# First chunk of sparse attention: exponentials of one sub-chunk moved to ScalarE, value loads reordered, one grouped product split up

## The chip, the cores and the metric

The program runs on one core of a Trainium2 chip. The metric is the device time of one launch in microseconds (us). Three timed runs of the kernel before gave 618.30, 618.59 and 619.15 us; the median is 618.59.

## The reference

For two batches of 576 positions and eight heads of width 64, four heads attend to the last 32 positions ("local") and four to the positions with the same remainder modulo 32 ("strided"), with a softmax in float32. The 1152 x 512 result x then goes through dense products:

```
scores = q @ k.T / 8, masked;  attn = exp(scores - max);  attn /= sum(attn) + 1e-9
x   = attn @ v                                 # 1152 x 512
x   = ((x @ w1) * (x @ w2)) @ w3 @ w_out        # 512 -> 1024 -> 1024 -> 512
out = sum over e of p[:, e] * (relu(x @ e1[e]) @ e2[e])    # 4 experts
```

## The kernel before

The order of the work on every engine is written out by hand, from line 828 on; each engine runs its own instructions in that order and semaphores join them. The change touches the beginning only: the attention of batch 0 and the loads around it.

That attention has six chunks, 0 to 2 local and 3 to 5 strided. For each chunk TensorE (PE) multiplies queries and keys into a PSUM bank (`scores`); VectorE (DVE) takes row maxima (`maxima`, L407), subtracts them into an SBUF frame (`subtract`, L415), ScalarE (ACT) takes exponentials (`exps`, L421), DVE sums and inverts (`sums`, L439 to L445), GpSimd (POOL) multiplies by the inverse (`normalise`, L449). PE transposes the frame (`transposes`, L454), ACT copies the transposes to SBUF (`evac`, L459), PE multiplies them by the values (`pv`, L475, L483 or L492), and ACT copies the products into `x_whole` (`put`, L526). The chunks are staggered, as lines 921 to 974 list them. Batch 1 does the exponentials in another way (`slots_exps`, L423 to L429): ACT reads the scores from PSUM with minus the maximum as its bias, one instruction for each of the six or eight slots, and gives the slot's sum with it.

Chunk 0's product is `paired`: 12 matmuls with 64 x 128 values as weights, of whose result half is used, the first six on one half of the rows and the next six on the other. Chunks 1 and 2 have 24 matmuls on 64 x 64 weights, in turn on the four quarters of the array. A float32 matmul stands as two instructions in the trace.

`keep_warm` (L114) has PE multiply zeros by zeros, so that it is not idle while it waits; nothing reads the result. Two such fillers of 512 columns stand between the first scores.

Nearly all loads are issued by SyncE (SP), in program order, each behind the one before. The queries and keys of the local heads come first (L830, with the queries from ACT's queue), then the values of chunk 0 (three loads), queries and keys of the strided heads (L841), the values of chunks 1 and 2 (four loads) and the strided values (`load_v_str`, `load_v_rest`, L844 and L845). Later, after the scaling of chunk 2, come the first dense weights `w12[0]` in two halves (`whole_load`, L149) and the next weights. `hold` has POOL write one column of a tile, so that the load into it waits for POOL's place in the order.

The dense part follows: `whole_product` (L590) multiplies batch 0's x by `w12[0]` in float32 with no split, in two halves of the weights; each half first takes `whole_low` on ACT and the five `whole_steps` on DVE. The next weights, `w12[1]`, are split in two parts by ACT and DVE, and from L1011 on, `run_unit` does the rest in three products each, with batch 1's attention between them.

Of the kernel before, what the change touches and what calls it, by code (L numbers as in the profile page):

```python
# [14 lines left out]
ALU = mybir.AluOpType  # L15
# [4 lines left out]
W = 32  # L20
# [17 lines left out]
def flat(ap):  # L38
    return ap.rearrange("p a b -> p (a b)")
# [3 lines left out]
def kernel(  # L43
# [13 lines left out]
    nc = tc.nc  # L57
# [14 lines left out]
    def bank(name):  # L72
        return ps.tile([P, 512], F32, tag="ps", name=name)
# [33 lines left out]
    def warm_up():  # L107

        idle = tmp.tile([P, P], F32, tag="pT", name="idle")
        nc.vector.memset(idle, 0.0)  # L110
        nc.scalar.activation(small.tile([P, 1], F32, tag="rec", name="one"), idle[:, :1], AF.Exp)
        moving = idle.unsqueeze(1).to_broadcast([P, 4, P])

        def keep_warm(n):  # L114
            if n:
                acc = bank("idle").rearrange("p (a b) -> p a b", a=4)
            for i in range(n):
                mm(acc, idle, moving, start=i == 0, stop=i == n - 1)

        keep_warm(WARM)  # L120
        return keep_warm
# [6 lines left out]
    class Chunk:  # L128
# [20 lines left out]
        def whole_load(self):  # L149
            nonlocal live  # L150
            live += 1
            self.raw = rawp.tile([P, 1024, 2], I32, tag="raw", name="raw64")
            self.t = unit("w_whole", I32)
            self.f32 = self.t.bitcast(F32)
            hold(True, self.raw[:, 0, :1])
            for i in range(2):
                c = slice(512 * i, 512 * i + 512)
                nc.sync.dma_start(out=flat(self.raw[:, c]), in_=self.src.bitcast(I32)[:, 1024 * i:1024 * i + 1024])

        def whole_low(self, i):  # L160
            c = slice(512 * i, 512 * i + 512)
# [158 lines left out]
                queue.dma_start(out=t[:, :, c], in_=src[b, pairs, :, c].rearrange("k p n -> p k n"))  # L320
        qk[b, g] = (tq, tk)

    def load_v_loc(b, c):

        tv = wp.tile([P, 2, 3, P], F32, tag="w", name="tv_loc")

        def load(dst, rows, t0, n):
            nc.sync.dma_start(out=dst, in_=v_loc[b, :, rows, t0:t0 + n].rearrange("k p t d -> p k t d"))

        lower, upper, middle = slice(0, 64), slice(64, P), slice(W, 3 * W)  # L330
        if c == 0:
            load(tv[lower, :, 0:1], lower, 0, 1)
            load(tv[upper, :, 0:1], middle, 0, 1)
            load(tv[:, :, 1:], slice(0, P), 1, 2)
        elif c == 1:
            load(tv, slice(0, P), 3, 3)
        else:
            load(tv[lower, :, 0:1], lower, 0, 1)
            load(tv[lower, :, 1:], middle, 1, 2)
            load(tv[upper], middle, 3, 3)  # L340
        vals[b, 0, c] = tv
# [11 lines left out]
    def load_v_rest(b):  # L353
        for k in range(2):
            nc.sync.dma_start(out=vals[b, 1][64 * k:64 * k + NB, 10:], in_=v_str[b, k, 2 * T3:2 * T3 + NB, :2])

    class Chunk4:
# [3 lines left out]

        def __init__(self, index, b, g, c):
            self.index, self.b, self.g, self.c = index, b, g, c
            self.paired = b == index == 0
            if g == 0:

                self.blocks = [9 * c + 3 * f + 2 * h if c < 2 else 3 * f + 9 * h + 1 for f in range(3) for h in range(2)]
                self.frames, self.nk = 3, 2 * W
            else:

                if c < 2:
                    self.groups = [(RS[t][0] + 3 * h, 3, 5 * h + t) for t in (2 * c, 2 * c + 1) for h in range(2)]
                else:
                    self.groups = [(RS[4][0] + 3 * h, 3, 5 * h + 4) for h in range(2)]
                    self.groups += [(RS[t][0] + 6, 1, 10 + t) for t in range(2)]
                self.frames, self.nk = 4, T3
            self.slots = 2 * self.frames
# [83 lines left out]
        def pv(self):  # L461

            if self.index == 3 and not self.b:
                banks = [ps_sc.tile([P, 512], F32, tag="sc", name="o") for _ in range(2)]
            else:
                banks = [bank("o") for _ in range(2)]
            if self.paired:
                tv = vals[self.b, 0, self.c]
                self.o = [o[:, :12 * W].rearrange("p (k f j q) -> p k f j q", k=2, f=3, j=2) for o in banks]
                pT = self.pT.rearrange("p (f k j q) -> p f k j q", f=3, k=2, j=2)  # L470
                for h in range(2):
                    r = slice(64 * h, 64 * h + 64)
                    for f in range(3):
                        for k in range(2):
                            mm(self.o[h][:, k, f], tv[r, k, f], pT[r, f, k], start=True, stop=True)  # L475
            elif self.g == 0:
                tv = vals[self.b, 0, self.c]
                self.o = [o[:, :6 * W].rearrange("p (k f q) -> p k f q", k=2, f=3) for o in banks]
                pT = self.pT.rearrange("p (f k j q) -> p f k j q", f=3, k=2, j=2)
                todo = [(f, k, h, j) for f in range(3) for k in range(2) for h in range(2) for j in range(2)]  # L480
                for f, k, h, j in todo:
                    r, d = slice(64 * h, 64 * h + 64), slice(64 * j, 64 * j + 64)
                    mm(self.o[h][d, k, f], tv[r, k, f, d], pT[r, f, k, j], start=True, stop=True)  # L483
            else:
                self.o = [o[:, :self.frames * T3].rearrange("p (f q) -> p f q", q=T3) for o in banks]
                pT = self.pT.rearrange("p (f j q) -> p f j q", j=2, q=2 * W)
                for f, (_, n, at) in enumerate(self.groups):
                    n = NB * n
                    for h in range(2):
                        for j in range(2):  # L490
                            r, d = slice(64 * h, 64 * h + n), slice(64 * j, 64 * j + 64)
                            mm(self.o[h][d, f, :n], vals[self.b, 1][r, at, d], pT[r, f, j, :n], start=True, stop=True)  # L492

        def puts(self):

            t0 = self.b * S
            to = (x_hi, x_lo) if self.b else (x_whole,)
            for h, o in enumerate(self.o):
                if self.g == 0:
                    at = self.blocks[h], self.blocks[2 + h] - self.blocks[h]  # L500
                    x = [x[:, :2, t0:t0 + S].rearrange("p k (i q) -> p k i q", q=W)
                         [:, :, at[0]:at[0] + 2 * at[1] + 1:at[1]] for x in to]
                    if self.paired:
                        for j in range(2):
                            d = slice(64 * j, 64 * j + 64)
                            yield o[d, :, :, j], [x[d] for x in x]
                    else:
                        yield o, x
                else:
                    x = [x[:, 2 + h, t0:t0 + S].rearrange("p (b r) -> p r b", r=W) for x in to]  # L510
                    r0 = self.groups[0][0]
                    parts = o.rearrange("p f (r b) -> p f r b", b=NB)
                    if self.c == 0:
                        for i in range(2):
                            yield (parts[:, 2 * i:2 * i + 2].rearrange("p f r b -> p (f r) b"),
                                   [x[:, 7 * i:7 * i + 6] for x in x])
                    else:
                        n = 4 if self.c == 1 else 2
                        yield parts[:, :n].rearrange("p f r b -> p (f r) b"), [x[:, r0:r0 + 3 * n] for x in x]
                    if self.c == 2:  # L520
                        yield parts[:, 2:, 0], [x[:, 6:14:7] for x in x]
# [306 lines left out]
    with tc.manual_schedule():  # L828
# [8 lines left out]
        make_identity(nc, ident)  # L837
        strided_masks()
        x_whole = big[1].tile([P, 4, S], F32, tag="big", name="x_whole")
        load_v_loc(0, 0)  # L840
        load_qk(0, 1)  # L841
        load_v_loc(0, 1)
        load_v_loc(0, 2)
        load_v_str(0)  # L844
        load_v_rest(0)  # L845
        zero = c_w12[0]
        rest_loads = {5: [lambda: load_qk(1, 1)], 6: [lambda c=c: load_v_loc(1, c) for c in range(3)],
                      8: [lambda: load_v_str(1), lambda: load_v_rest(1)]}
# [58 lines left out]

        def scale_of(i):
            first[i].sums()
            first[i].normalise()  # L910

        def put(i):
# [10 lines left out]
        exp_of(0)  # L923
        keep_warm(1)
        first[2].scores()
        exp_of(1)
        scale_of(0)
        keep_warm(1)
        first[3].scores()
        first[0].transposes()  # L930
        first[4].scores()
        exp_of(2)
        scale_of(1)
        evac(0)
        first[1].transposes()
        first[5].scores()
# [14 lines left out]
        load_next(True)  # L951
        first[3].transposes()
        first[2].pv()
        evac(3)
        put(1)
        first[3].pv()
        scale_of(5)
        load_qk(1, 0, held=True)
# [1 line left out]
        put(2)  # L960
        first[4].transposes()
        evac(4)
        first[5].transposes()
        zero.whole_low(0)
        zero.whole_steps(0)
# [219 lines left out]
```

## Time and profile before

| | |
|---|---|
| median of three runs | 618.59 us |
| the profiled execution | 620.32 us |
| its span, first to last instruction | 618.4 us |
| mean granted clock of TensorE | 0.994 |
| PE busy | 613.7 us, 99% of the span |
| DVE busy, ACT busy | 442.9 us (72%), 278.5 us (45%) |
| POOL busy | 9.8 us |

The page counts an engine as busy while an instruction of its own runs. The granted clock is TensorE's share of its full speed: 1.00 is 2.4 GHz, 0.50 is 1.2 GHz. The chain of waits is followed back from the last instruction, at each step to what released it. All times within the span count from its first instruction.

### The profile page before, as it was taken

How to read it: one execution, taken by the hardware profiler on the slowest of the kernel's cores; microseconds unless marked ns; L12 is line 12 of the kernel's file. 1: busy time of each engine (PE TensorE's matmuls, PEld its weight loads, DVE VectorE, ACT ScalarE, POOL GpSimd, SP SyncE). 2: the span in 40 equal slices, each digit the busy share in tenths (PEclk: the TensorE clock that was granted, in tenths of full speed). 3: DMA queues.
4: the chain of work that ended last, by engine and by line, in shares of the span. 5: the costliest groups of instructions: out<-in, count | busy, mean ns of one | idle time of the engine just before them, and what ended most of it. 6: DMA issues, size and time to landing. Idle time of an engine off the chain costs nothing.

```text
span 618.4 us, 11234 instructions
## 1 busy us (share of the span) xinstructions
PE 613.7 (99%) x4558; PEld 559.5 (90%) x4558; DVE 442.9 (72%) x797; ACT 278.5 (45%) x545; POOL 9.8 (2%) x33
## 2 busy tenths in 40 slices
PE   9999999999999999999999999999999999999997
PEld 5889999998889999999899998899989898989997
DVE  5799986898864236777877987887766665755843
ACT  3779965666643225333343344443333333333320
POOL 4100000000000000000000000000000000000000
PEclk9799999999999999999999999999999999999999
DMA  9987340244523011333445344445585556465411
GB/s 273 315 305 206 112 165 2 77 136 169 196 105 127 32 48 62 136 143 137 166 174 179 121 178 151 166 160 189 187 315 215 208 200 238 170 229 182 146 58 69
DMA packets 28511, 99.64 MB, mean 161 GB/s; under 512 B 2660, under 2 KB 6316, under 8 KB 26028
## 3 DMA queue, kind: packets, MB, share of 16 engines
q1 hardware_dynamic: 27916, 98.34, 45.3%
q8 instruction: 36, 0.59, 0.4%
q10 hardware_dynamic: 544, 0.59, 0.3%
q14 instruction: 15, 0.12, 0.1%
HBM read 79.78 MB, written 19.14 MB: 160 GB/s over the span
## 4 chain that ended last, share of the span: by engine, by line
PE 93%; DVE 3%; DMA 2%; ACT 2%; issue 1%; SPq 0%; DVEq 0%
PE g_acc L303 11%; PE g_acc L304 11%; PE g_acc L305 11%; PE m_a L305 4%; PE m_a L304 4%; PE m_a L303 4%; PE ab_acc L303 3%; PE ab_acc L304 3%; PE ab_acc L305 3%; PE m_b L304 3%; PE m_c L303 3%; PE x_acc L305 3%; PE x_acc L303 3%; PE x_acc L304 3%; PE m_c L304 3%; PE m_b L303 3%
## 5 line engine op out<-in xcount | busy, mean ns | idle before, releaser
L737 ACT ACTIVATE h_hi<-u 128x320 fp32r<-128x320 f32 (+1 forms) x128 | 56.9, 445 | 189.4 <-DVE u L743 189.4
L303 PE MATMUL g_acc<-w_hi,h_hi 128*128 128x512 f32 (+1 forms) x296 | 114.3, 386 | 0.0
L304 PE MATMUL g_acc<-w_lo,h_hi 128*128 128x512 f32 (+1 forms) x296 | 114.2, 386 | 0.0
L305 PE MATMUL g_acc<-w_hi,h_lo 128*128 128x512 f32 (+1 forms) x296 | 113.7, 384 | 0.0
L676 DVE TENSOR_TENSOR w_lo<-raw,w_hi 128x768 fp32r<-128x768 f32 x64 | 69.4, 1084 | 12.4 <-ACT w_hi L674 12.4
L743 DVE TENSOR_TENSOR u<-m_b,u 128x320 f32<-128x320 f32 (+1 forms) x96 | 40.8, 452 | 50.7 <-PE m_b L305 50.6
L303 PE MATMUL ab_acc<-x_hi,w_hi 128*128 128x288 f32 x240 | 71.6, 298 | 0.2 <-ACT ab L578 0.2
L305 PE MATMUL ab_acc<-x_hi,w_lo 128*128 128x288 f32 x240 | 70.7, 294 | 0.0
L304 PE MATMUL ab_acc<-x_lo,w_hi 128*128 128x288 f32 x240 | 70.7, 294 | 0.0
L305 PEld LDWEIGHTS g_acc<-w_hi,h_lo 128*128 128x128 f32 x296 | 55.6, 188 | 11.6
L303 PEld LDWEIGHTS g_acc<-w_hi,h_hi 128*128 128x128 f32 x296 | 55.8, 188 | 8.0
L304 PEld LDWEIGHTS g_acc<-w_lo,h_hi 128*128 128x128 f32 x296 | 55.7, 188 | 7.6
L739 DVE SCALAR_TENSOR_TENSOR h_lo<-u,h_hi 128x320 fp32r<-128x320 f32 (+1 forms) x128 | 57.6, 450 | 3.7 <-ACT h_hi L737 1.9
L674 ACT CAST w_hi<-raw 128x768 fp32r<-128x768 f32 x64 | 59.9, 936 | 0.0
L303 PEld LDWEIGHTS ab_acc<-x_hi,w_hi 128*128 128x128 f32 x240 | 45.0, 188 | 0.7 <-ACT ab L578 0.4
L304 PEld LDWEIGHTS ab_acc<-x_lo,w_hi 128*128 128x128 f32 x240 | 45.0, 188 | 0.0
L305 PEld LDWEIGHTS ab_acc<-x_hi,w_lo 128*128 128x128 f32 x240 | 45.0, 188 | 0.0
L304 PE MATMUL m_b<-b_t,s_hi 128*128 128x320 f32 (+1 forms) x128 | 37.9, 296 | 0.0
L743 DVE TENSOR_TENSOR u<-m_a,u 128x320 f32<-128x320 f32 (+1 forms) x64 | 28.9, 451 | 11.6 <-PE m_a L305 11.6
L676 DVE TENSOR_TENSOR s_lo<-raw,s_hi 128x1024 fp32r<-128x1024 f32 x16 | 19.6, 1226 | 24.3 <-ACT s_hi L674 24.3
L743 DVE TENSOR_TENSOR u<-m_c,u 128x320 f32<-128x320 f32 (+1 forms) x64 | 28.9, 452 | 4.9 <-PE m_c L305 3.9
L753 ACT COPY u<-m_a 128x320 f32<-128x320 f32 (+1 forms) x32 | 12.8, 400 | 41.9 <-PE m_a L305 41.9
(179 smaller groups left out, 1420.4 us busy)
## 6 DMA issues: line engine op xcount, KB each, us to landing
raw<-in_e_dram SPq DMA_DIRECT2D x32, 1024.0 KB, 5.1
raw<-in_w3T_dram SPq DMA_DIRECT2D x8, 1024.0 KB, 5.0
stored<-s_hi SPq DMA_DIRECT2D x16, 512.0 KB, 2.6
stored<-s_lo SPq DMA_DIRECT2D x16, 512.0 KB, 2.7
s_hi<-stored SPq DMA_DIRECT2D x16, 512.0 KB, 3.6
s_lo<-stored SPq DMA_DIRECT2D x16, 512.0 KB, 4.9
raw<-in_w_dram SPq DMA_DIRECT2D x7, 1024.0 KB, 7.2
raw<-in_w_out_dram SPq DMA_DIRECT2D x4, 1024.0 KB, 4.8
```

The lines of the kernel that those rows point to most:

```text
L303: mm(acc, lh, rh, start=first, stop=False)
L304: mm(acc, lh, rl, start=False, stop=False)
L305: mm(acc, ll, rh, start=False, stop=last)
L674: nc.scalar.copy(dst[0], src)
L676: nc.vector.tensor_tensor(out=dst[1], in0=src, in1=dst[0].bitcast(F32), op=ALU.subtract)
L737: nc.scalar.activation(hi, src, AF.Relu)
L739: nc.vector.scalar_tensor_tensor(out=lo, in0=src, scalar=0.0, in1=hi.bitcast(F32), op0=ALU.max, op1=ALU.subtract)
L743: nc.vector.tensor_tensor(out=out, in0=acc, in1=b, op=ALU.add)
L753: nc.scalar.copy(u1, a)
```

## The change

Six edits, all within the first 40 us or so. Chunk 1 of batch 0 takes the way of batch 1 (`slots_exps` on ACT, `recip` afterwards), so its `subtract` and its sum leave DVE, and its reciprocal and scaling come behind `exp_of(2)` in the order. The local values are asked for behind chunk 0's reciprocal: POOL first writes one column of their tile from that reciprocal, so the queries and keys of the strided heads go ahead of them. The strided values are asked for between the two halves of `w12[0]`. Chunk 0's product and its `put` become those of the other local chunks. The second filler has 256 columns, not 512, and a new one of 256 stands between the transposes of chunks 4 and 5. `put(1)` comes ahead of `evac(3)`.

```
-        def keep_warm(n):
+        def keep_warm(n, parts=4):
...
-                mm(acc, idle, moving, start=i == 0, stop=i == n - 1)
+                mm(acc, idle, moving[:, :parts], start=i == 0, stop=i == n - 1)
...
                 nc.sync.dma_start(out=flat(self.raw[:, c]), in_=self.src.bitcast(I32)[:, 1024 * i:1024 * i + 1024])
+                if i == 0:
+                    load_v_str(0)
+                    load_v_rest(0)
...
-    def load_v_loc(b, c):
+    def load_v_loc(b, c, behind=None):
         tv = wp.tile([P, 2, 3, P], F32, tag="w", name="tv_loc")
+        if behind:
+            nc.gpsimd.tensor_tensor(out=tv[:, 0, 0, :1], in0=behind.p[:, 0, :1], in1=behind.rec[:, :1], op=ALU.mult)
...
-            if self.paired:
...
-                for h in range(2):
-                    r = slice(64 * h, 64 * h + 64)
-                    for f in range(3):
-                        for k in range(2):
-                            mm(self.o[h][:, k, f], tv[r, k, f], pT[r, f, k], start=True, stop=True)
-            elif self.g == 0:
+            if self.g == 0:
...
-        load_v_loc(0, 0)
         load_qk(0, 1)
-        load_v_loc(0, 1)
-        load_v_loc(0, 2)
-        load_v_str(0)
-        load_v_rest(0)
...
         def scale_of(i):
             first[i].sums()
+            if i == 0:
+                load_v_loc(0, 0, first[0])
+                load_v_loc(0, 1)
+                load_v_loc(0, 2)
             first[i].normalise()
...
-        exp_of(1)
+        first[1].maxima()
+        first[1].slots_exps()
         scale_of(0)
-        keep_warm(1)
+        keep_warm(1, 2)
...
         exp_of(2)
-        scale_of(1)
+        first[1].recip()
+        first[1].normalise()
...
         first[2].pv()
+        put(1)
         evac(3)
-        put(1)
...
         evac(4)
+        keep_warm(1, 2)
         first[5].transposes()
```

## Rows read from the trace of the kernel before

**Rows 1.** The page, section 2: granted clock of TensorE, in tenths, in 40 slices.
```profile
PEclk9799999999999999999999999999999999999999
```

**Rows 2.** Stretches: us, busy PE, PEld, DVE, ACT, POOL, then granted clock, DMA, GB/s.
```profile
18.00:18.50 0.50, 0.50 (x45) 0.50 (x37) 0.00 (x0) 0.48 (x3) 0.50 (x1) 0.89 0.75 270
...
25.00:26.00 1.00, 1.00 (x37) 0.91 (x34) 0.93 (x4) 1.00 (x6) 0.00 (x0) 0.89 1.00 352
```

**Rows 3.** The chain of waits, 7 to 34 us: start, us, what, how many.
```profile
7.30 1.06 PE idle L118 x2
...
9.33 1.06 PE idle L118 x2
...
14.91 2.43 PE o L475 x24
17.33 0.48 PE tp L454 x3
17.81 0.94 PE o L483 x48
18.75 1.04 PE tp L454 x4
19.80 1.44 PE o L483 x48
21.23 0.89 PE o L492 x32
22.12 1.90 PE tp L454 x8
24.02 1.83 PE o L492 x64
25.85 7.96 PE ab_acc L593 x32
```

**Rows 4.** Waits of PE and of its weight loads: total us, times, longest.
```profile
PE sc L390 <- DMA tqk<-in_qT_dram: 0.3, 1, 0.3
...
PEld sc L401 <- DMA tqk<-in_qT_dram: 0.6, 1, 0.6
```

**Rows 5.** The timeline of DVE, SP and ACT: start, duration, instruction.
```profile
1.74 2.00 SPq L328 DMA_DIRECT2D tv_loc<-in_v_loc_dram  x3
...
8.02 0.56 DVE L415 TENSOR_TENSOR p_ring<-sc,mx 128x384 f32<-128x384 f32 x1
...
10.53 0.54 DVE L439 TENSOR_REDUCE rec<-p_ring 128x6 f32<-128x384 f32 x1
...
10.65 0.52 ACT L421 ACTIVATE p_ring<-p_ring 128x384 f32<-128x384 f32 x1 [1.50 <-DVE p_ring L415]
...
14.75 2.16 SPq L158 DMA_DIRECT2D raw<-in_w_dram  x2
...
18.65 0.33 SPq L138 DMA_DIRECT2D raw<-in_w_dram  x1
...
27.34 1.19 ACT L147 ACTIVATE t<-raw 128x1024 f32<-128x1024 f32 x1
...
35.44 1.35 DVE L552 TENSOR_TENSOR x_lo<-x_whole,x_hi 128x1152 fp32r<-128x1152 f32 x1
```

**Rows 6.** The timeline of ACT, one local chunk of batch 1 by slots.
```profile
47.42 0.20 ACT L425 ACTIVATE mx<-mx 128x6 f32<-128x6 f32 x1
...
49.12 0.34 ACT L428 ACTIVATE p_ring<-sc,mx 128x64 f32<-128x64 f32 x1
```

**Rows 7.** Two stretches of loads, the last column GB/s.
```profile
7.50:10.50 3.00, 3.00 (x54) 1.24 (x53) 2.72 (x7) 0.69 (x2) 0.83 (x1) 1.00 1.07 393
11.50:15.50 4.00, 3.96 (x80) 3.16 (x78) 3.69 (x9) 2.08 (x4) 1.80 (x5) 1.00 1.07 219
```

**Rows 8.** DMA issues of short stretches: KB each, us to landing.
```profile
raw<-in_w_dram SPq DMA_DIRECT2D x1, 512.0 KB, 4.1
...
raw<-in_w_dram SPq DMA_DIRECT2D x1, 1024.0 KB, 6.4
```

More of the change, by code (lines that the diff above doesn't have):

```diff
@@ L112, in warm_up @@
         moving = idle.unsqueeze(1).to_broadcast([P, 4, P])
-        def keep_warm(n):
+        def keep_warm(n, parts=4):
             if n:
-                acc = bank("idle").rearrange("p (a b) -> p a b", a=4)
+                acc = bank("idle").rearrange("p (a b) -> p a b", a=4)[:, :parts]
             for i in range(n):
-                mm(acc, idle, moving, start=i == 0, stop=i == n - 1)
+                mm(acc, idle, moving[:, :parts], start=i == 0, stop=i == n - 1)
         keep_warm(WARM)
@@ L363, in __init__ @@
             self.index, self.b, self.g, self.c = index, b, g, c
-            self.paired = b == index == 0
             if g == 0:
@@ L466, in pv @@
                 banks = [bank("o") for _ in range(2)]
-            if self.paired:
-                tv = vals[self.b, 0, self.c]
-                self.o = [o[:, :12 * W].rearrange("p (k f j q) -> p k f j q", k=2, f=3, j=2) for o in banks]
-                pT = self.pT.rearrange("p (f k j q) -> p f k j q", f=3, k=2, j=2)
-                for h in range(2):
-                    r = slice(64 * h, 64 * h + 64)
-                    for f in range(3):
-                        for k in range(2):
-                            mm(self.o[h][:, k, f], tv[r, k, f], pT[r, f, k], start=True, stop=True)
-            elif self.g == 0:
+            if self.g == 0:
                 tv = vals[self.b, 0, self.c]
@@ L502, in puts @@
                          [:, :, at[0]:at[0] + 2 * at[1] + 1:at[1]] for x in to]
[L503 to L508, printed above, removed]
+                    yield o, x
                 else:
```

## The prediction

> **What bounds the kernel now.** I read the page first: PE is busy for 613.7 of 618.4 us (the table above), and its clock is below nine tenths in one slice of 40, the second [rows 1]. Something to win can therefore only be work that PE need not do or does at half speed, and the second slice, 15 to 31 us, is where to look. The windows show the slow stretch: the clock falls within the half microsecond from 18.0 and is back shortly after 25.0 [rows 2]; by their means of 0.89 it stood at 0.50 from 18.4 to 25.3, that is 6.8 us. The chain of waits shows what PE did there [rows 3]. Before the fall came chunk 0's product, 24 instructions in 2.43 us; chunk 1 does the same sums with 48 instructions in 0.94. The waits list shows that PE hardly stands still for anybody: 0.3 us for the second half of the local queries, 0.6 us of a weight load for the strided ones [rows 4]. Behind the attention the chain is PE again: whole products at 25.85, and then the first split products, just when DVE has done the last part of x, 35.44 + 1.35 = 36.79 us [rows 5].
>
> **The change part by part.** The profiled execution took 620.32 us, 1.92 more than its span and 1.73 more than the median of the runs; I work out a difference within its span and take it off the median. The place that I follow is the start of the whole products, 25.85.
>
> *Chunk 0's product.* 12 wide matmuls become 24 narrow ones that use the four quarters of the array in turn. By the chunk 1 row: 0.94 for 2.43, so **-1.49 us** of PE, on the path. Its `put` falls from four ACT copies to two; nothing waits for them.
>
> *Fillers.* A full one is 1.06 us [rows 3], a half 0.53. One is halved, one half is added: **0**. The strided scores can use the earlier start because their queries no longer queue behind chunk 0's values: the wait of 0.6 us before them shows the coupling, and without 0.38 MB ahead they land 1.0 us earlier at 393 GB/s [rows 4, 7].
>
> *The clock.* With the wide product gone, PE goes through tighter work. If the fall does not come, the rows at half clock shrink: four transposes from 1.04 to 4/3 of 0.48, -0.40; chunk 2 from 1.44 to 0.94, -0.50; chunk 3 from 0.89 by the same ratio to 0.58, -0.31; eight transposes from 1.90 to 1.28, -0.62; of chunks 4 and 5 the 1.25 us before 25.3, -0.43 [rows 3]. Sum **-2.26 us**. What the trace shows of it: ahead of the return stood the eight transposes and most of chunks 4 and 5; ahead of that, with the clock staying low, four transposes and chunks 2 and 3. So the stretch with more transposes is the one that brought it back. The Trainium skill (TensorE: Matmul & The Clock Gate, "Part 4: PE-mode transpose") says that transposes do not count as busy for the clock in the same way as matmuls; by that rule the new order, with the same transposes on a shorter path, would keep its slow stretch, which is the second rival below. The trace speaks rather against the rule.
>
> *Chunk 1's exponentials.* DVE loses a subtraction (0.56) and a sum (0.54) [rows 5]; ACT gets a copy and six slots, 47.42 to 49.46, 2.04 us [rows 6], for one exponential. They run from 8.0, where the maxima are there, to about 10.1, on an ACT that next has chunk 2's exponential at 10.65 [rows 5], so nobody waits. The subtraction was between chunk 1's maxima and chunk 0's sum: chunk 0's reciprocal comes some 0.5 us earlier, and so does DVE's further list, which has no gap up to chunk 5. Worth 0 on PE's path by itself, but it moves POOL's scalings, and the loads held behind them, 0.5 us ahead.
>
> *Local values behind the reciprocal.* POOL's added column is one more small instruction ahead of a scaling that is 0.5 us early. Three loads issued from about 9.1 take SP 2.0 us [rows 5]. The fixed part of a load is 4.1 us less what another 512 KB cost, 6.4 - 4.1 = 2.3, so 1.8 [rows 8]; the third is issued at some 10.5 and lands at 10.5 + 1.8 + 0.7 of bytes = 13.0, or at 10.5 + 4.1 = 14.6 if it takes as long as the 512 KB. Chunk 0's product is due at 14.91 - 0.53 - 0.5 = 13.9. Cost 0 to 0.7; I take 0, since there is no backlog.
>
> *Local queries.* The strided keys now follow them at once, in place of small value loads. PE already waits for the second half of the queries [rows 4], and these come by ACT's queue, against which SP's larger transfers now compete. Price between 0 and 0.9 (0.38 MB more at 393 GB/s in the way); I take **+0.2**.
>
> *Strided values between the halves.* This is the edit that costs. They were asked for right behind the local values and needed at 21.23; now they follow the first half of the weights, which POOL's place in the order lets go at 14.75 - 0.54 = 14.2 [rows 5]. That half is down at 14.2 + 1.8 + 1.3 = 17.3. Then 0.66 MB: at 393 GB/s down at 19.0, at 219 GB/s at 20.3, and if the half takes the 4.1 of its row, at 21.3 [rows 7, 8]. The slow rate stood while these same loads, each to 64 partitions, ran. The Trainium skill (SBUF — State Buffer, "Door 1: The DMA port swizzle") has loads to 64 partitions reach half of the ports and so half of the rate, which makes 219 a property of the loads rather than of that moment's crowd; by the crowd's reading it would be 19.0. I take 20.0, nearer to the slow end. Without a wait chunk 3's product would start at 21.23 - 1.49 - 0.53 - 0.40 - 0.50 + 0.2 = 18.5. **Wait +1.5** (0.5 to 2.8). Under it lies `evac(3)`, which now stands behind `put(1)` and would else cost 0.3.
>
> *Sum*: -1.49 - 2.26 + 0.2 + 1.5 = **-2.05 us**; products start at 23.8. Is the rest ready? Chunk 4's transposes end at 21.2; their copy, `whole_low` and DVE's last step on the first half of the weights come to some 2 us as estimated from the operations of like size in [rows 5]: 23.2, in time. The weights `w12[1]`, whose magnitude ACT took at 27.34 [rows 5], were asked for at 18.65 and landed 6.4 later [rows 5, 8]; by 0.5 us earlier that is 24.5, so DVE's list to the split products can move by at most 2.8 us. PE's 2.05 is less, and it carries to the end, since PE has no wait to take it up.
>
> **Rivals.**
> - *Values in time* (0.13): the strided loads land by 18.5. For: the old queue was crowded there, the new is not. Against: the 219 row. Then the bound of 2.8 from `w12[1]` decides: 615.8.
> - *The clock falls all the same* (0.25): the wait for the values makes a hole that the old order did not have, so eight transposes, the filler and chunks 4 and 5 run at half: 0.62 + 0.53 + 0.43 = 1.6 back. -0.45, 618.1. For: PE was called busy without a break before the fall too. Against: the wide product is gone.
> - *Slower* (0.12): the hole lets the clock fall only as the whole products begin, and for as long as before. 6.8 us at half clock over work that fills PE cost 3.4 us: -2.05 + 3.4 = +1.35, 619.9. It decides when the strided values land after some 20 us, so that the fall comes after chunks 4 and 5 rather than ahead of them.
> - *The local values come late* (0.08): chunk 0 waits the 0.7: -1.35, 617.2.
>
> **How the numbers follow.** Forecast 618.59 - 2.05, rounded, 616.6, chance 0.42; its own range is 615.8 to 617.4 by the bounds of the wait. The range for 8 in 10 reaches over the second rival and into the third, and down to the rival with no wait and 0.8 below it: 615.0 to 619.3. What a measurement can tell from no change is 0.2%, 1.24 us. Faster: 0.39 of the forecast, 0.12, 0.04 and 0.03 of the first, second and fourth rival, 0.58. Slower: 0.05 of the second and 0.10 of the third, 0.15. The same: 0.27.
>
> **What would show it.** After, the chain should have chunk 0's product in 0.9 to 1.0 us; granted clock 1.00 in 18 to 26; a wait of PE for the strided values of 0.5 to 2.8 us ahead of chunk 3; whole products at 23.8 and the first split product 2 us earlier than 36.85. The prediction is wrong if the clock is at 0.50 under the whole products, if the scores of chunk 1 start over 0.5 us later, or if a later wait (DVE's last part of x) eats the gain.

## The result, and the profile after

The changed kernel takes 624.85 us, the median of four runs (624.39 to 625.37), where the kernel before took 618.87 on the same chip. The ratio is 1.0089, with a 95% interval of 1.0070 to 1.0108: slower by about 5.5 us by the ratio; the two medians by themselves lie 5.98 apart. Forecast were 616.6 us, 2 us faster. Two runs at a much lower clock (1002 us with all loads back, 749 us with the local values back) are left out of the medians below.

The profiled execution took 625.37 us with a span of 623.3. Its page: the busy line, the granted clock in 40 slices, and the queue that carries instructions (packets, MB, share).

```profile
PE 612.6 (98%) x4584; PEld 558.7 (90%) x4584; DVE 441.7 (71%) x795; ACT 279.2 (45%) x555; POOL 9.9 (2%) x34
...
PEclk9699999999999999999999999999999999999999
...
q8 instruction: 36, 0.59, 0.4%
```

PE has 1.1 us less to do than before and ends 4.9 us later. The clock is lower than in [rows 1], and in the same slice, so this slice is again where to look. The waits of PE in the first 45 us, and the longest of SP's queue there:

```profile
PE o L487 <- DMA tv_str<-in_v_str_dram: 4.2, 2, 2.6
PE sc L394 <- DMA tqk<-in_qT_dram: 1.1, 1, 1.1
PE idle L118 <- DVE idle L110: 1.0, 1, 1.0
PE o L478 <- issue: 0.7, 1, 0.7
...
SPq L333 <- POOL tv_loc L330: 8.0, 1, 8.0
```

Against [rows 4], 0.3 us for the local queries has become 1.1, the strided values are waited for twice, 4.2 us together, and in chunk 1's product (L478) PE stands for 0.7 us with nothing recorded that it waits for. SP does nothing for 8.0 us: it waits for the column that POOL writes into the tile of the local values. The chain of waits of the changed kernel (start, us, what, how many), against [rows 3]:

```profile
7.92 0.87 PE sc L394 x48
...
17.32 8.35 DMA tv_str<-in_v_str_dram
25.66 0.14 issue
25.80 1.10 PE o L487 x28
26.90 1.04 PE tp L458 x4
27.95 0.85 PE idle L118 x2
28.80 0.85 PE tp L458 x4
29.65 1.53 PE o L487 x64
31.19 6.03 PE ab_acc L583 x24
```

A DMA, not PE, now sets the time from 17.32 to 25.67, and the whole products start at 31.19, 5.34 us later than before. From the timeline of the changed kernel (start, us, instruction; in brackets the idle time before it and what ended it):

```profile
10.46 0.19 POOL L330 TENSOR_TENSOR tv_loc<-p_ring,rec 128x1 f32<-128x1 f32 x1 [5.12 <-DVE rec L449]
...
10.67 4.46 SPq L333 DMA_DIRECT2D tv_loc<-in_v_loc_dram  x7
...
16.19 1.74 SPq L355 DMA_DIRECT2D tv_str<-in_v_str_dram  x2
...
18.48 0.42 PE L478 MATMUL o<-pT,tv_loc 64*64 64x32 f32 x11 [0.75 <-issue]
...
19.42 1.73 PE L478 MATMUL o<-pT,tv_loc 64*64 64x32 f32 x48
23.77 0.46 PE L487 MATMUL o<-pT,tv_str 54*64 54x54 f32 x4 [2.62 <-DMA tv_str<-in_v_str_dram]
```

Chunk 2's product ends at 19.42 + 1.73 = 21.15; before, at 21.23 [rows 3]. Up to there the two are level: what chunk 0's narrow product (1.57, from 2.43 to 0.86) and the halved filler (0.43) saved has gone into the later scores (1.49) and the stop in chunk 1's product (0.75). The whole loss lies behind it: 10.04 us to the whole products where there were 4.62. Of the 5.42 more, 4.19 are the two waits for strided values (2.62 above, 1.57 ahead of the 28 at 25.80), 0.85 the new filler at half clock, and 0.37 the products of chunks 3 to 5, 3.09 for 2.72. The first split product follows the whole products by 11.0 us in both kernels, at 42.2 for 36.85, and nothing further on takes the loss up.

Two groups of stretches of the changed kernel, the clock and the loads (us, busy engines, granted clock, DMA share, GB/s):

```profile
9.00:12.00 3.00, 3.00 (x70) 1.67 (x71) 2.24 (x6) 2.09 (x13) 1.02 (x2) 1.00 0.00 0
12.00:16.00 4.00, 4.00 (x134) 3.28 (x132) 3.56 (x11) 2.06 (x5) 1.80 (x5) 1.00 0.77 226
16.00:20.00 4.00, 3.03 (x94) 2.38 (x91) 3.29 (x8) 2.92 (x8) 2.23 (x5) 1.00 0.86 229
20.00:24.00 4.00, 1.38 (x48) 1.28 (x41) 1.44 (x4) 0.71 (x3) 0.58 (x2) 0.50 1.07 205
...
20.00:21.00 1.00, 1.00 (x44) 1.00 (x37) 0.00 (x0) 0.17 (x1) 0.58 (x2) 0.51 1.10 204
...
30.00:31.00 1.00, 1.00 (x60) 0.94 (x52) 0.93 (x3) 1.00 (x6) 0.00 (x0) 0.87 1.16 446
```

From 9 to 12 us not one byte is loaded; before, the same stretch moved 334 GB/s. What stands in SP's order up to the strided values (1152 KB of local ones, 512 KB of weights, 676 KB of strided ones) is 2.40 MB, and at some 225 GB/s from 12.0 it takes 10.7 us: down at 22.7 at the earliest, since the second half of the weights shares the time. They landed at 23.6 and 25.7, the first weights at 22.4 and 26.9, the next, `w12[1]`, at 29.4 (25.0 before). The clock was at 0.50 from 20.02 to 30.26, 10.2 us where it had been 6.8; it fell while PE was in chunk 2's product, 1.1 us ahead of the first wait for strided values.

### The profile page after: what moved, and what is told of

Same layout as the page of the kernel before. It is cut to its first block, busy times and chain, and to the rows that moved or that the text cites. A ratio compares the mean times of both kernels' runs of the same rounds, so it can differ in the third digit from the quotient of the medians.

```text
span 623.3 us, 11294 instructions
## 1 busy us (share of the span) xinstructions
PE 612.6 (98%) x4584; PEld 558.7 (90%) x4584; DVE 441.7 (71%) x795; ACT 279.2 (45%) x555; POOL 9.9 (2%) x34
## 4 chain that ended last, share of the span: by engine, by line
PE 91%; DVE 3%; DMA 2%; ACT 2%; issue 1%; SPq 0%; POOL 0%; DVEq 0%; ACTq 0%
PE g_acc L306 11%; PE g_acc L307 11%; PE g_acc L308 11%; PE m_a L308 4%; PE m_a L307 4%; PE m_a L306 4%; PE ab_acc L306 4%; PE ab_acc L307 4%; PE ab_acc L308 4%; PE m_b L307 3%; PE m_c L306 3%; PE x_acc L308 3%; PE x_acc L306 3%; PE x_acc L307 3%; PE m_c L307 3%; PE m_b L306 3%
```

## The experiments

**All loads back at their old places** (the arithmetic edits alone).

```
-                if i == 0:
-                    load_v_str(0)
-                    load_v_rest(0)
...
+        load_v_loc(0, 0)
         load_qk(0, 1)
+        load_v_loc(0, 1)
+        load_v_loc(0, 2)
+        load_v_str(0)
+        load_v_rest(0)
...
-            if i == 0:
-                load_v_loc(0, 0, first[0])
...
```

> The changed kernel with every load at its old place in the order (values of chunk 0 ahead of the strided queries, the other local and the strided values behind them); the other edits stay. Theory A, the late values cost the time (PE waits for them and its clock then stays at half for longer): 615 to 617 us, no wait of PE for values, products near 23 us in the span. Theory B, the strided queries and keys pushed ahead crowd the second half of the local queries (PE's first long wait went from 0.3 to 1.1 us and all started 1.5 us later): also below 618.9, with scores of chunk 1 at 6.4. Theory C, the thinner fillers and the new order of the arithmetic make the clock fall for longer: 620 us or more.

619.38 us against 619.53; ratio 0.9997 (0.9980 to 1.0013), so none of the three theories had the time. All that costs is in the loads. What should have brought something, chunk 0's narrow product, brings nothing either: in chunk 1's product PE stands 0.84 us, with 11 of its 48 instructions to go, and the whole products start at 25.88, where [rows 3] has 25.85.

**Strided values back alone**, right behind the strided queries; local ones stay behind the reciprocal.

```
-                if i == 0:
-                    load_v_str(0)
-                    load_v_rest(0)
...
         load_qk(0, 1)
+        load_v_str(0)
+        load_v_rest(0)
```

> The changed kernel with only the strided values back ahead of the local ones, right behind the strided queries; the local values stay behind the reciprocal. Theory A: the 4.2 us of waiting for strided values are gone and the half clock is shorter, 618 to 621 us. Theory B: the late start of 1.5 us stays and is all that counts, 623 us or more.

620.18 us; ratio 1.0015 (0.9990 to 1.0040). By the ratios the strided values' place is worth 1.0089 / 1.0015, 0.74%, of the 0.89%. SP waits for POOL's column here too, but with the strided values asked for ahead of that wait the loads run at 200 GB/s from 9 to 12, and the products start at 25.78. Theory A holds.

**Local values back alone**; the strided ones stay between the halves.

```
+        load_v_loc(0, 0)
         load_qk(0, 1)
+        load_v_loc(0, 1)
+        load_v_loc(0, 2)
...
-            if i == 0:
-                load_v_loc(0, 0, first[0])
...
```

> The changed kernel with the local values back at their old places, ungated; the strided values stay between the halves of the first weights. Theory A: the strided values land about as late behind POOL's hold, at 20 to 23 us, so 1 to 3 us of waiting stay: 619 to 623 us. Theory B: the scores of chunk 1 start at 6.4 again and the time is at 620 or below whatever the strided values do.

623.10 us, the median of three; ratio 1.0063 (1.0045 to 1.0081), just above what theory A allowed. There is no profile of it to read, so where its time goes isn't shown.

**The strided values' move alone, on the kernel before.**

```
+                if i == 0:
+                    load_v_str(0)
+                    load_v_rest(0)
...
-        load_v_str(0)
-        load_v_rest(0)
```

> The kernel before with only the strided values moved between the two halves of the first weights. Theory A: PE gets to chunk 3 at 21.2 and the values land at 20 to 23: 0 to 2 us of waiting, 619 to 622 us. Theory B: no change, 618.5 to 619.5 us.

623.80 us; ratio 1.0073 (1.0055 to 1.0091): this one edit makes as much as the other way round, and more than either theory had. Stretches and chain of this kernel:

```profile
9.00:12.00 3.00, 3.00 (x85) 2.01 (x77) 2.74 (x10) 1.04 (x2) 0.83 (x1) 1.00 1.09 340
12.00:16.00 4.00, 3.36 (x74) 2.56 (x73) 3.46 (x8) 1.79 (x4) 1.79 (x5) 1.00 0.14 32
```

```profile
15.84 3.66 PE o L478 x24
...
28.76 6.03 PE ab_acc L596 x24
```

The loads run dry here as well, only from 12 to 16 us (32 GB/s): what had filled that time were the strided values, and the next load, the weights, is held until POOL's place. But PE waits for no strided value in this trace; it runs at half clock from 16.79 to 27.03, chunk 0's wide product in 3.66 us for 2.43. So one and the same edit shows itself once as a wait of 4.2 us and once as slow clock alone. The slow clock may hide a wait: PE reached chunk 3's product at 24.25, at full clock some 3.7 us sooner (an estimate, half of the 7.46 us from 16.79), and the first strided load landed only at 21.4.

**The kernel before once more**, to see whether its slow stretch belongs to it. No edit.

> The kernel before, unchanged, for a second look at it in an execution whose mean clock is 1.000 (most of its timed runs have that; the profiled one had 0.994). If the half-clock stretch at 18 to 25 us was an accident of the profiled execution: span near 616.7 us, clock 1.00 throughout, whole products starting 1.5 to 2.3 us before 25.8. If it is the rule: span 618.4 and the same stretch.

619.06 us, span 617.1, and the page has the clock at full speed in all 40 slices. That line, and two of its chain:

```profile
PEclk9999999999999999999999999999999999999999
...
21.17 1.04 PE tp L454 x8
...
24.37 6.03 PE ab_acc L593 x24
```

The eight transposes took 1.04 us for the 1.90 of [rows 3], and the products start 1.5 us earlier. The slow stretch on which my largest term rested belongs to that execution, not to every one. Of 69 timed executions of the kernel before, 47 have a mean clock of 0.999 or 1.000 (median 619.03 us), and 15 have 0.994 or 0.995 (median 620.89) like the one that I read, at 620.32.

**Chunk 0's narrow product alone, on the kernel before.**

```
-            if self.paired:
...
-                            mm(self.o[h][:, k, f], tv[r, k, f], pT[r, f, k], start=True, stop=True)
-            elif self.g == 0:
+            if self.g == 0:
...
-                    if self.paired:
...
+                    yield o, x
```

> The kernel before with chunk 0's product and its put made like those of the other chunks, nothing else. By the prediction's step: 1.5 us less of PE on the path, 617.0 to 617.5 us. By the theory that PE's instructions come in blocks of 16 KB, which PE reaches sooner than they are loaded once the work is made of many small matmuls: PE stands 0.5 to 1.0 us with no data missing in chunk 1's product, and the time is within 0.5 us of the kernel before.

619.19 us; ratio 0.9989 (0.9967 to 1.0011). Its chain:

```profile
16.23 0.70 PE o L473 x37
16.93 1.19 issue
18.13 0.42 PE o L473 x11
...
22.52 0.84 issue
...
24.38 9.66 PE ab_acc L578 x32
```

The product is done 1.6 us sooner, and then PE stops for 1.19 us with 11 of chunk 1's 48 to go, and once more for 0.84 later. The products start at 24.38; in the unchanged kernel at full clock, 24.37. The saving is real and all of it is given back. In this profile the clock then falls under the whole products: it is at 0.50 from 24.8 to 28.2, and they take 9.66 us for the 7.96 of [rows 3], in a kernel with every load at its old place.

**Where the stops come from**: six matmuls of four columns more in the warm-up of that kernel, so that everything behind stands 12 instructions further down PE's list (a float32 matmul is two).

```
         keep_warm(WARM)
+        tiny = bank("idle")[:, :4]
+        for i in range(6):
+            mm(tiny, idle, idle[:, :4], start=i == 0, stop=i == 5)
```

> The kernel before with the narrow product of chunk 0 (as in the run with that alone, where PE stood 1.2 us in chunk 1's product with 11 of 48 instructions left), and six matmuls of four columns added to the warm-up, where PE waits for queries anyway. If PE stands because its instructions come in blocks and the next block is not there: the same stop comes six matmuls earlier in the list, with 23 of 48 instructions left. If it stands for data (values, banks, copies): it stays at 11 left.

622.01 us in the one run; a pair of fillers takes 2.00 us at 10.83 and 1.05 at 13.88, so PE worked at half speed for longer at the start. What counts is where PE stops. Its chain, and below it the stop ahead of that one in the kernel with the strided move alone:

```profile
17.30 0.47 issue
17.76 0.60 PE sc L403 x15
...
21.02 0.52 PE o L476 x25
21.54 0.20 issue
21.75 0.55 PE o L476 x23
```

```profile
13.40 0.64 issue
14.04 0.30 PE sc L404 x3
```

The stop moved from 11 to go to 23 to go, and the next stop ahead of it, in chunk 4's scores, from 3 to go (so in the kernel with the strided move alone) to 15: 12 in both. So the stops sit at fixed places of PE's own list, not at a datum that is late. Counted through the traces (matmuls, weight loads and semaphore instructions), each of the 15 stops of over 0.15 us, in ten kernels, stands behind entry 449, 705 or 961 of the list: 256 apart. The trace has packets of 16,384 bytes on the instruction queue (36 of them make the 0.59 MB of the page's row); 36 times 256 is 9,216, and the list of the kernel before has 9,201 entries. In the kernel with the narrow product alone they took 1.3 and 1.8 us between the value loads, and at 14 of the 15 stops PE went on 1.3 to 1.8 us after one had landed (0.9 at the other). The packets don't name the engine that they are for, so that PE waits for them is still a reading, if a close one; the fixed places are shown. The Trainium skill (Runtime: NRT & Kernel Launch, "Instruction fetch mechanics") has an engine's list refilled in 16 KiB blocks, at a cost that is mostly hidden; the block's size agrees with the row, the hiding doesn't here, with 1.19 and 0.84 us in the open.

**Strided queries ahead of chunk 0's values, on the kernel before.**

```
-        load_v_loc(0, 0)
         load_qk(0, 1)
+        load_v_loc(0, 0)
```

> The kernel before with the strided queries and keys asked for ahead of chunk 0's values, nothing else. If they crowd the second half of the local queries: that half lands at about 7.8 in place of 6.3 us, the scores of chunk 1 start 1.2 to 1.6 us later, and the time is 0.5 to 1.5 us above the kernel before. If that half is late for another reason: scores of chunk 1 at 6.4 and no change.

620.81 us; ratio 1.0020 (1.0000 to 1.0041). The scores of chunk 1 started at 7.11, where the kernel before once more had 6.95 and my profile of it 6.43. Six profiles with the old order of these loads have 6.43 to 6.95 (median 6.80), six with the strided queries first 7.11 to 7.92 (median 7.25): some 0.45 us later, not the 1.5 between my two first profiles. Not all of it need be crowding, as the scores of chunk 0 before them took 1.44 us in some profiles and 0.87 in others. With the 0.15% left in the second experiment, all that stays beside the strided move is about 0.2%, at the edge of what the runs tell.

**Strided values behind the local ones**, with these behind the reciprocal, instead of between the halves.

```
-                if i == 0:
-                    load_v_str(0)
-                    load_v_rest(0)
...
                 load_v_loc(0, 2)
+                load_v_str(0)
+                load_v_rest(0)
```

> The changed kernel with the strided values asked for right behind the local ones, not between the halves of the first weights. If being held behind those weights makes them late: they land 2 to 3 us earlier, near 21 to 22 us, PE waits 1 to 2 us in place of 4.2, and the time is 621 to 623 us. If the local values in front of them (loads to half of the partitions, slow) make them late: no change, 624 to 625 us.

622.67 us; ratio 1.0053 (1.0034 to 1.0072). Waits of PE:

```profile
PE o L484 <- DMA tv_str<-in_v_str_dram: 0.4, 1, 0.4
PE ab_acc L580 <- DVE w_whole L174: 0.3, 1, 0.3
```

The strided values now cost 0.4 us of waiting, but the first half of the weights lands at 23.8 and the whole products wait for it, through DVE, until 26.79. The order within the queue only chooses who is late; from 9 to 12 us this kernel loads at 22 GB/s.

**Strided values in one load over 128 partitions**, not two over 64, on the kernel before and on the changed one (the values lie otherwise in memory).

```
-        for k in range(2):
...
-            nc.sync.dma_start(out=tv[64 * k:64 * k + 64, :10].rearrange("p (h t) d -> p h (t d)", h=2), in_=rows)
+        nc.sync.dma_start(out=tv[:, :10], in_=v_str[b, :, :10])
```

> The kernel before with the strided values of each batch laid out for one load to 128 partitions in place of two to 64 (the same bytes in the tile). If loads to half of the partitions are slow in themselves (219 GB/s while they run): that stretch goes at 350 to 400 GB/s, the values land 1 to 2 us earlier and the first weights too; the time is 617 to 618.9 us. If they were slow for what else was under way: 219 GB/s stays and no change.

On the kernel before: 619.47 us; ratio 0.9992 (0.9972 to 1.0012). Its stretch while these loads run, and the same of the kernel before once more:

```profile
12.00:14.50 2.50, 2.50 (x58) 1.84 (x58) 2.40 (x6) 1.49 (x3) 1.10 (x3) 1.00 1.08 304
```

```profile
12.00:14.50 2.50, 2.50 (x48) 1.82 (x47) 2.36 (x7) 1.19 (x3) 1.03 (x3) 1.00 1.08 232
```

304 GB/s for 232: the slow rate of [rows 7] belongs to how these loads are laid out and not to the crowd, as I took it. The Trainium skill (SBUF — State Buffer, "Door 1: The DMA port swizzle") says that 64 partitions reach half of the ports; the two rows agree with it in direction, not by its factor. The new layout also has fewer and longer packets, 602 for 729 from 11 to 16 us, and no run parts the two. The time gains nothing that can be measured, since nothing waits for these values there.

> The changed kernel with the strided values in one load to 128 partitions, still between the halves of the first weights. By the half-partition theory the values land 1.3 to 2 us earlier, PE's wait falls from 4.2 to 2 to 3 us, and the time from 624.9 to 622 to 623.5 us. By the theory that it is the empty stretch of the queue from 9 to 12 us that counts, the gain is under 0.7 us.

On the changed kernel: 624.31 us; ratio 1.0069 (1.0050 to 1.0088). The wait:

```profile
PE o L484 <- DMA tv_str<-in_v_str_dram: 1.1, 1, 1.1
```

1.1 us for 4.2, and `w12[1]` at 27.1 for 29.4, of which 0.6 is POOL's column that came earlier in this execution (9.83 for 10.46); the ratio falls by 0.2%, less than the intervals can tell apart. The clock stands in the way: its ten runs have means of 0.989 to 0.997.

**PE kept busy through the wait**: three fillers of 512 columns ahead of chunk 3's product in the changed kernel.

```
         evac(3)
+        keep_warm(3)
         first[3].pv()
```

> The changed kernel with three more fillers of 512 columns (3.2 us) where PE waits for the strided values, ahead of chunk 3's product. If the hole in PE's work is what takes its clock to half for 10 us: the stretch is shorter or gone, the mean clock 0.995 or more, and the time 622 to 624 us. If the clock falls for what PE did earlier: 0.992 and 624 to 626 us, the fillers hidden in the wait.

623.31 us; ratio 1.0057 (1.0039 to 1.0076). Stretches of it:

```profile
20.00:21.00 1.00, 1.00 (x44) 0.83 (x37) 0.00 (x0) 0.48 (x3) 0.07 (x2) 0.99 1.05 221
...
24.00:25.00 1.00, 1.00 (x3) 0.14 (x1) 0.00 (x0) 0.00 (x0) 0.00 (x0) 0.81 1.01 410
```

The clock falls at 20.97, as the fillers begin right behind chunk 2's product, but is back at 24.39, not at 30.26; the ten runs have mean clocks of 0.994 to 1.000, the four of the changed kernel 0.992. Four of the ten runs have a mean clock of 1.0, and a median of 622.75 us: 3.7 above the 619.03 of the kernel before at the same clock. That much the changed kernel loses without any such stretch, with the fillers and the later scores in it; the rest up to 624.85, some 2 us, I put down to the clock.

## Why the prediction was wrong, point by point

The sum had the whole products start 2.05 us earlier, and in the profile they start 5.34 later. The step that failed first is the wait for the strided values; the clock's term and chunk 0's saving fell away as well.

- *The strided values between the halves* is the step that decided. It put the landing at 20.0 (19.0 to 21.3) and the wait at 1.5 (0.5 to 2.8); measured were 23.6 and 25.7, and 4.2. I had the right rate, but counted behind the first half of the weights alone and took the local values to be landed ("no backlog"). They were not: chunk 1's and 2's four loads stand behind the reciprocal too, I priced three loads where SP issues seven (4.46 us), and the stream in front was empty from 9 to 12. The 2.40 MB in order from 12.0 at the 219 of [rows 7] would have said 23.0 or later. The same omission made `w12[1]` 24.5 where it was 29.4. That this edit makes 0.63 to 0.74% of the 0.89% is shown three ways (local values back, the edit alone, strided values back).
- *The clock, -2.26.* The largest term, and mostly not there to be had: the execution read was slower by 1.73 us than the median largely because of that stretch (its span is 618.4 us, 617.1 without it), and I carried these 1.73 as a constant between profile and median. In two of three executions the kernel before has no such stretch. The second rival (the clock falls all the same) and the third (the hole lets it fall) come nearer: it fell at 20.0 and stayed low for 10.2 us. But it fell ahead of the hole, in chunk 2's product, and it covered the wait and chunks 3 to 5, not the whole products; the fillers, in one profile and ten mean clocks, speak for the hole making it last, not for its making it fall. No run tests the transposes rule weighed in the prediction: in the kernel before once more, eight transposes passed at a clock of 1.00, in 1.04 us.
- *Chunk 0's product, -1.49*: right in size (0.86 us, from 15.48, with no wait for values) and worth nothing at the products' start, because PE's list then stops at a fixed place that the slow product had hidden. I had asked which engine is late next, not whether PE's own instructions are.
- *Local queries, +0.2*: chunk 1's scores started 1.5 us later in the changed kernel's profile (7.92 for 6.43), beyond the bound of 0.9. Over six profiles of either order it is 0.45, within the bound: the rest is two single executions. The reciprocal that the loads now hang on stands behind chunk 1's maxima on DVE, so later scores hold up the loads too: POOL's column came at 10.46 (9.68 to 9.95 in the other four kernels that have it), not at some 9.1.
- *Chunk 1's exponentials, the fillers, `put(1)`*: nothing, as said; all loads back gives 0.9997.
- *Local values late (the fourth rival)*: no. The first of chunk 0's loads landed at 13.1, and its product began at 15.48 without a wait. Close to it, though: with the strided values of the changed kernel in one load, PE waited 0.8 us for a local value in chunk 1's product.
- The slower rival had the right sign, with 619.9 as its price; it knew the hole and the clock and not the late loads behind them. Without a stretch at half clock the changed kernel, fillers added, still loses 3.7 us.

What stays open: why the clock of the kernel with the strided move alone falls (all four runs at 0.989 to 0.997) when PE waits for nothing recorded, and so how its 0.73% divides into clock and loads; why one execution has the stretch and the next has not; and whether the stops of PE, which stand ahead of the fall in several of these profiles, have a part in it.

## What to carry to other kernels

A queue of loads is one stream: before moving one, add up the bytes that stand in order ahead of it from the moment the stream can run, at the rate that the profile shows, and look for the stretch that the move leaves empty. A load that is held by a computation holds everything behind it. And a term taken from one profiled execution, a slow-clock stretch above all, needs a second execution before it is counted, since the median may never have had it.

## What the runs showed of the hardware

- Stretches of many small matmuls stop at fixed places of PE's instruction list, for 0.2 to 1.4 us, and 12 instructions more ahead of them moved two such places by exactly 12. Counted with the weight loads, the places are 256 entries apart, and PE goes on 0.9 to 1.8 us after a packet of 16,384 bytes has landed. Work taken out just ahead of such a place is waited for there.
- The mean clock of one and the same program varies between executions, 0.992 to 1.000 over the 69 of the kernel before, and 0.994 for 0.999 or more goes with 1.9 us. With the strided values behind the local ones' gate or between the halves it was never above 0.997 (31 runs of five kernels), except with fillers in the wait.
- A stretch of 3 us without a byte loaded, 9 to 12, came back as lateness of the loads behind it: `w12[1]` landed at 29.4 for 25.0 in the changed kernel. With the strided move alone, dry from 12 to 16, it landed at 27.7.
